# Level products two to five read 32 columns of R with a stride in place of all 64

## The chip, the cores and the metric

The kernel runs on one core of a Trainium2 chip. The metric is the device time of one execution in microseconds (us); lower is better. In what follows PE is TensorE, PEld its weight loads, DVE is VectorE, ACT is ScalarE, POOL is GpSimd and SP is SyncE, whose queue issues most DMAs.

## The reference

The kernel computes a linear attention with a decaying state and, on its output, a gated two-layer network. Batch is 4, heads 8, sequence 768, head dimension 48; the network has width 384 and 2048 hidden units. All is fp32.

```python
for t in range(S):
    cur = np.einsum('bhd,bhe->bhde', u[None] * kt, vt)
    y[:, :, t] = np.einsum('bhd,bhde->bhe', rt, state + cur)
    state = wt[:, :, :, None] * state + np.einsum('bhd,bhe->bhde', kt, vt)
# x: y as (3072 tokens, 384)
h = x @ w_in
sp = np.maximum(h, 0.0) + np.log1p(np.exp(-np.abs(h)))
out = (h * erf(sp)) @ w_out
```

So a query r of token t meets the key k of an earlier token s with all the decays w between them multiplied on.

## The kernel before

**Steps.** The work is cut into 12 steps: 6 chunks of 128 tokens times 2 pairs of batches. A step holds 16 heads (2 batches of 8). Two heads lie on each tile's partitions, the even head's 48 dimensions from partition 0 and the odd head's from partition 64, so that a tile has 8 such pairs (`n`) of 128 tokens. `in_t[:, 0]` is R (queries) and `in_t[:, 1]` is K (keys), both with tokens along the free dimension.

**Levels.** Inside a chunk each half of 64 tokens is treated by halving. At level l the tokens fall into blocks of 2^l; in each block the keys of the left half meet the queries of the right half. `scale` (L309, its instruction is at L332) multiplies the right halves of R and the left halves of K, in place, by the decays up to the middle of the block, so that at the next level the products carry the right decays. Per level, then:

- `level_products` (L536, matmuls at L544): for each of the 8 pairs, each half `s0` of the chunk and each of the two heads `e`, one matmul with 64 tokens of K as weights and tokens of R as the moving operand, into a PSUM tile `pp`. These are 32 matmuls, each of which the profile shows as two records with a weight load each. At levels 1 to 5 all 64 columns of K meet all 64 columns of R, at level 6 the left 32 of K meet the right 32 of R.
- `scale` for this level, on VectorE. It overwrites what the matmuls read, so it waits for them.
- `take_level` (L552): at levels 2 to 5 a masked copy on VectorE (L556) takes from `pp` the elements of this level into `own`, the 64 x 64 matrix of each head. It goes over the right halves of the columns only (`rights`, L52), 512 elements a partition, for `own`, for the mask and for `pp`. At level 6 ScalarE copies instead (L563). At level 1 the whole `pp` is multiplied by a mask (L896).

Steps 0 to 3 (`attend_first`, L739, and `attend`, L862) do levels 1 to 6; level 1 takes R and K with u multiplied in (`rk1`). Step 4 does levels 4 to 6, steps 5 to 11 (`attend_late`, L686) levels 5 and 6. There the low levels are done another way, by products on VectorE and POOL of rows of tokens (L467, L471) summed at L457, and `own` starts from these sums (L518).

Then `from_own` (L569, matmuls at L578) multiplies `own` by the values v, `through_state` (L592, L604) adds what comes from the state, and `state_part` (L643, L652) makes the new state. `spread_blocks` (L660, L665) is a small product of step 4 and later. `keep_busy` (L853, L857) issues matmuls of zeros in step 0.

**The network beside it.** The hidden layer (L1006) and the output layer (L1038 in the first steps, L1114 later) of earlier steps are cut into pieces, and pieces are put between the stages of the attention, in steps 1 to 4 by fixed tables (`STAGES`, `beside`, `in_order`), later by strings of tokens (`LATE`, `USUAL`). In steps 1 to 3 the weights are also brought into fp32, by ACT (L252, L254, L260), VectorE (L269, L274) and POOL (L282).

**Order.** All of this stands inside `tc.manual_schedule` for all five engines: each engine runs its instructions in the order in which the program names them, and waits only for what its operands need.

Of the kernel before, what the change touches and what calls it, by code (L numbers as in the profile page):

```python
# [20 lines left out]
HC = 64  # L21
# [22 lines left out]
MASKED = 5  # L44
# [7 lines left out]
def rights(ap, half):  # L52

    names = "abcdefg"[: len(ap.shape) - 1]
    spread = " ".join(names)
    return ap.rearrange(f"{spread} (n two h) -> {spread} n two h", two=2, h=half)[
        (slice(None),) * len(names) + (slice(None), 1)
    ]
# [3 lines left out]
def kernel(  # L62
# [237 lines left out]
    def rows(e, n=D):  # L300
        return slice(e * EP, e * EP + n)
# [234 lines left out]
    def level_products(pp, rk, level, ns=range(NJ * NP)):  # L536

        half = 1 << (level - 1)
        m = HC if level <= MASKED else half
        for n in ns:  # L540
            for s0 in range(0, C, HC):
                for e in range(NE):
                    t0 = s0 if level <= MASKED else s0 + half
                    nc.tensor.matmul(  # L544
                        pp[s0 : s0 + m, e, n, :m],
                        lhsT=rk[rows(e), 1, n, s0 : s0 + m],
                        rhs=rk[rows(e), 0, n, t0 : t0 + m],
                        start=True,
                        stop=True,
                    )  # L550

    def take_level(own, pp, level):  # L552
        half = 1 << (level - 1)
        got = pp[:].rearrange("p e n t -> p (e n) t")
        if level <= MASKED:
            nc.vector.copy_predicated(  # L556
                rights(own[:], half),
                rights(mask_sb[:, level - 1 : level, :].to_broadcast([P, NH, HC]), half),
                rights(got, half),
            )  # L560
        else:
            for s0 in range(0, C, HC):
                nc.scalar.copy(own[s0 : s0 + half, :, half:], got[s0 : s0 + half, :, :half])  # L563
# [122 lines left out]
    def attend_late(s, run):  # L686
# [4 lines left out]
        if before:  # L691
            from_own(before, ready[before][0], 1)
            fence()
        pp = products([P, NE, JP, HC], 0)
        level_products(pp, RK, LOG - 1)
        scale(s, LOG - 1)
        take_level(own, pp, LOG - 1)
        run("front", None)
        if before:
# [16 lines left out]

        pp = products([P, NE, JP, HC], 0)
        level_products(pp, RK, LOG)
        if s + 1 < n_steps:
            spread_blocks(s + 1, pp)  # L720
        take_level(own, pp, LOG)
        scale(s, LOG)
        run(1, following)
# [15 lines left out]
    def attend_first(xT):  # L739
# [11 lines left out]
        for half in halves:  # L751
            level_products(pp, made[:], 1, half)
            stay_warm(2)
# [17 lines left out]
        for level in range(2, LOG):  # L771
            pp = turns.pop("pp", None) or products([P, NE, JP, HC])
            level_products(pp, RK, level)
            scale(0, level)
            turns["pp"] = products([P, NE, JP, HC])
            keep_busy(turns["pp"])
            take_level(own, pp, level)
            if level in behind:
                wait_for(1 << level - 1)
                totals(*behind[level])  # L780
            if level == 2:
                stages["b"](0, 0)
                stages["b"](0, 1)
                stages["r"](0)
                for _ in prepare(1):
                    pass
                stages["l"](1, own[:, 0, 2:3])
                nc.sync.dma_start(out=vt[:], in_=v[0])
                nc.sync.dma_start(out=ws[1][:], in_=rkw[1][:, 2])
                load_w(2)  # L790
                load_v(1)
            elif level < LOG - 1:
                stages["h"](0)
# [455 lines left out]
    for kk in range(KT):  # L1249
        n = D // KT  # L1250
        to, of = (x.rearrange("p (e m) -> p e m", e=NE) for x in (apart[:, kk], ident[:]))
# [181 lines left out]
```

## Time and profile before

| | us |
|---|---|
| median of 3 runs (lowest, highest) | 592.12 (592.08, 592.5) |
| the profiled execution, its own time | 592.82 |
| its span, first to last instruction | 591.0 |
| TensorE busy | 581.3 |
| TensorE, level products (L544), records of 64 columns of K and of R from `in` | 29.0 |
| the same, level 6 | 9.1 |
| TensorE, hidden layer (L1006) | 256.9 |
| VectorE busy | 436.5 |
| VectorE, L332 with `tot_sb` | 82.0 |
| VectorE, L556, 25 copies, mean 0.813 | 20.3 |

The span is that of the profiled execution, in which times inside the trace are counted from the first instruction. A line of the groups names the line of the kernel, the engine, the operation, what is written and read, the shapes, the count, then busy time and mean duration (ns) and the idle time before it with what ended it. Matmul ends are modelled, and matmuls overlap, so the duration of one is not the time that it takes of the engine; starts are what to count with.

A matmul's shape in these groups is that of the weights with a star (48*64 is 48 rows and 64 columns) and that of the moving operand with an x (48x64 is 48 rows and 64 columns).

### The profile page before, as it was taken

What the parts mean: (1) busy time and instruction counts of PE and PEld (TensorE: products, weight loads), DVE (VectorE), ACT (ScalarE), POOL (GpSimd) and SP (SyncE); (2) the same over time, 40 slices, a digit from 0 to 9 for tenths busy, and PEclk for the clock granted to TensorE, in tenths of its full rate; (3) what the DMA queues carried; (4) which work ended last, traced back from release to release, by engine and by line L of the source; (5) the groups of instructions that cost most, each with busy time, mean ns of one, the idle gap of its engine ahead of it and who ended that gap; (6) DMA issues with size and microseconds to landing.
All of it is one profiled execution on the core that took longest, in us unless ns stands there. A gap on an engine that the chain in (4) does not pass through costs nothing.

```text
span 591.0 us, 16616 instructions
## 1 busy us (share of the span) xinstructions
PE 581.3 (98%) x7264; PEld 499.1 (84%) x7264; DVE 436.5 (74%) x518; ACT 361.3 (61%) x474; POOL 270.7 (46%) x305
## 2 busy tenths in 40 slices
PE   8899999999999999999999999999999999999997
PEld 6687887678668768998998998998898898898997
DVE  6686886899996899799799799799799525033140
ACT  3558877644544597766766766766766754746710
POOL 3466381702398479469369369369369000000000
PEclk9999999999999999999999999999999999999999
DMA  7786571440442514334334334333331300000000
GB/s 242 235 277 235 196 238 55 167 153 10 143 118 96 134 42 160 48 126 162 63 128 155 67 129 150 72 128 115 73 114 47 73 22 14 3 24 10 2 28 27
DMA packets 53937, 63.24 MB, mean 107 GB/s; under 512 B 35144, under 2 KB 40424, under 8 KB 52840
## 3 DMA queue, kind: packets, MB, share of 16 engines
q1 hardware_dynamic: 53480, 61.98, 33.3%
q8 instruction: 57, 0.93, 0.7%
q10 hardware_dynamic: 384, 0.20, 0.1%
q14 instruction: 16, 0.13, 0.1%
HBM read 52.39 MB, written 8.69 MB: 103 GB/s over the span
## 4 chain that ended last, share of the span: by engine, by line
PE 89%; ACT 4%; DVE 3%; issue 2%; DMA 1%; ACTq 0%; SPq 0%; DVEq 0%
PE m L1006 42%; PE m L1114 28%; PE pp L544 6%; PE m L1038 5%; PE y L578 2%; PE pp L652 2%; PE y L604 2%; DVE in L332 1%; ACT room L962 1%; PE pp L917 1%; ACT L966 1%; DMA u_sb<-in_u 1%; ACT L962 0%; DVE rk L467 0%; ACTq L638 0%
## 5 line engine op out<-in xcount | busy, mean ns | idle before, releaser
L1006 PE MATMUL m<-xT,w_in_sb 128*128 128x256 f32 x1152 | 256.9, 381 | 0.8 <-ACT o L1047 0.6
L1006 PEld LDWEIGHTS m<-xT,w_in_sb 128*128 128x128 f32 x1152 | 216.1, 190 | 31.7 <-ACT o L1047 1.0
L1015 ACT COPY h<-m 128x512 f32<-128x512 f32 x96 | 55.7, 580 | 83.7 <-PE m L1006 83.7
L332 DVE TENSOR_TENSOR in<-in,tot_sb 128x1024 f32<-128x1024 f32 (+1 forms) x59 | 82.0, 1390 | 17.0 <-PE pp L544 14.4
L467 POOL TENSOR_TENSOR rk<-words 128x528 f32<-128x528 f32 (+3 forms) x28 | 42.5, 1517 | 92.1 <-DVE sums L457 81.7
L471 POOL TENSOR_TENSOR words<-words,rest 128x528 f32<-128x528 f32 (+10 forms) x77 | 78.2, 1015 | 6.0
L1038 PE MATMUL m<-w_out_sb,h 128*128 128x384 f32 x192 | 64.3, 491 | 0.0
L1038 PEld LDWEIGHTS m<-w_out_sb,h 128*128 128x128 f32 x192 | 35.7, 190 | 23.6
L1114 PE MATMUL m<-mixed,h 128*128 128x192 f32 x288 | 51.1, 331 | 0.0
L1114 PE MATMUL m<-w_out_sb,h 128*128 128x192 f32 x288 | 50.3, 329 | 0.0
L962 ACT ACT_TABLE_LOAD x36 | 46.2, 1283 | 3.2 <-issue 2.5
L1114 PEld LDWEIGHTS m<-w_out_sb,h 128*128 128x128 f32 x288 | 46.9, 190 | 0.5
L1114 PEld LDWEIGHTS m<-mixed,h 128*128 128x128 f32 x288 | 46.6, 190 | 0.9
L966 ACT ACT_TABLE_LOAD x36 | 46.2, 1283 | 1.6 <-DVE room L1097 1.1
L1114 PE MATMUL m<-w_out_sb,room 128*128 128x192 f32 x256 | 44.2, 326 | 0.0
L544 PEld LDWEIGHTS pp<-in 48*64 48x64 f32 (+1 forms) x2368 | 33.6, 126 | 11.9 <-issue 6.5
L1114 PEld LDWEIGHTS m<-w_out_sb,room 128*128 128x128 f32 x256 | 42.0, 190 | 0.0
L971 DVE TENSOR_TENSOR h<-h,y 128x1024 f32<-128x1024 f32 x17 | 20.7, 1215 | 28.3 <-ACT y L966 28.2
L544 PE MATMUL pp<-in 48*64 48x64 f32 (+1 forms) x2368 | 38.0, 212 | 1.2 <-DVE in L332 1.0
L962 ACT ACTIVATE room<-h 128x1024 f32<-128x1024 f32 x36 | 38.1, 1057 | 0.4
L406 POOL TENSOR_TENSOR tot_sb<-tot_sb 128x256 f32<-128x256 f32 (+4 forms) x50 | 36.2, 723 | 3.8
L971 DVE TENSOR_TENSOR h<-h,pp 128x1024 f32<-128x1024 f32 x19 | 23.0, 1213 | 20.0 <-ACT pp L966 19.9
(141 smaller groups left out, 814.9 us busy)
## 6 DMA issues: line engine op xcount, KB each, us to landing
in<-in_rkw SPq DMA_DIRECT2D x8, 1024.0 KB, 5.4
words<-in_moe_w_in SPq DMA_DIRECT2D x16, 384.0 KB, 4.7
words<-in_moe_w_out SPq DMA_DIRECT2D x16, 384.0 KB, 4.3
words<-in_rk_rows SPq DMA_DIRECT2D x8, 768.0 KB, 6.4
w<-in_rkw SPq DMA_DIRECT2D x11, 512.0 KB, 5.7
v<-in_v SPq DMA_DIRECT2D x12, 384.0 KB, 5.9
out<-o SPq DMA_DIRECT2D x24, 192.0 KB, 3.3
in<-in_rkw SPq DMA_DIRECT2D x7, 512.0 KB, 5.3
```

Source lines behind the costliest of these rows:

```text
L332: nc.vector.tensor_mul(halves, halves, view(tots[level - 1], 0, [[1, n], [2, nb], [0, half]]))
L406: nc.gpsimd.tensor_mul(new, pair[:, :, 0], pair[:, :, 1])
L467: engine.tensor_mul(terms[n], r[:, :, n:], k[:, :, : near - n])
L471: engine.tensor_mul(k[:, :, :m], k[:, :, :m], w[:, :, n : n + m])
L544: nc.tensor.matmul(pp[s0 : s0 + m, e, n, :m], lhsT=rk[rows(e), 1, n, s0 : s0 + m], rhs=rk[rows(e), 0, n, t0 : t0 + m], start=True, stop=True,)
L962: nc.scalar.activation(sp_room, chunks[0], AF.Softplus)
L966: nc.scalar.activation(at, sp_room, AF.Erf)
L971: nc.vector.tensor_mul(h, h, at)
L1006: nc.tensor.matmul(ps[:, ff, :], lhsT=w_in_sb[:, g * FG + f + ff, kk * P : (kk + 1) * P], rhs=xT[:, kk, :], start=kk == 0, stop=kk == KT - 1,)
L1015: nc.scalar.copy(h[:, f : f + FT, :], ps[:])
L1038: nc.tensor.matmul(ps[j][:], lhsT=gs[g][:, f, j * C : (j + 1) * C], rhs=w_out_sb[:, g * FG + f, :], start=g + f == 0, stop=g == NG - 1 and ...
L1114: nc.tensor.matmul(to, lhsT=a[:, f], rhs=b[:, f], start=start and f == 0, stop=f == FG - 1, skip_group_check=True,)
```

## The change

The products of levels 2 to 5 take as moving operand the right halves of R's blocks alone: 32 of 64 columns, in runs of 2 tokens at level 2, 4 at level 3, 8 at level 4 and 16 at level 5, each run followed by a gap of the same length. The weights stay 64 columns of K. The 32 result columns are written side by side into the first half of each row of `pp`, and the masked copy reads them there; `own` and the mask are still addressed with the stride. Level 1 stays as it is. Level 6 goes through the same code and reads and writes what it did before. The number of instructions stays the same.

```diff
         for n in ns:
             for s0 in range(0, C, HC):
                 for e in range(NE):
-                    t0 = s0 if level <= MASKED else s0 + half
+                    right = rk[rows(e), 0, n, s0 : s0 + HC]
+                    to = pp[s0 : s0 + m, e, n, :]
+                    if level > 1:
+                        right = rights(right, half)
+                        to = to[:, : HC // 2].rearrange("p (b h) -> p b h", h=half)
                     nc.tensor.matmul(
-                        pp[s0 : s0 + m, e, n, :m],
-                        lhsT=rk[rows(e), 1, n, s0 : s0 + m],
-                        rhs=rk[rows(e), 0, n, t0 : t0 + m],
+                        to, lhsT=rk[rows(e), 1, n, s0 : s0 + m], rhs=right,
                         start=True,
                         stop=True,
                     )
...
             nc.vector.copy_predicated(
                 rights(own[:], half),
                 rights(mask_sb[:, level - 1 : level, :].to_broadcast([P, NH, HC]), half),
-                rights(got, half),
+                got[..., : HC // 2].rearrange("p n (b h) -> p n b h", h=half),
             )
```

## The prediction, made before the result

> **What bounds the kernel now.** I read the page first: who is busy, and what the chain that ended last is made of.
>
> ```profile
> PE 581.3 (98%) x7264; PEld 499.1 (84%) x7264; DVE 436.5 (74%) x518; ACT 361.3 (61%) x474; POOL 270.7 (46%) x305
> ...
> PE 89%; ACT 4%; DVE 3%; issue 2%; DMA 1%; ACTq 0%; SPq 0%; DVEq 0%
> PE m L1006 42%; PE m L1114 28%; PE pp L544 6%; PE m L1038 5%; PE y L578 2%; PE pp L652 2%; PE y L604 2%; DVE in L332 1%; ACT room L962 1%; PE pp L917 1%; ACT L966 1%; DMA u_sb<-in_u 1%; ACT L962 0%; DVE rk L467 0%; ACTq L638 0%
> ```
>
> TensorE is the bound: it is 89% of the chain, and the level products (L544) are 6% of it, some 35 us. So a level product that really becomes shorter makes the kernel shorter. The 7264 weight loads (PEld) stand beside 7264 matmuls: each matmul has a load of its own. The question is which of the two sets the pace in a level product. The groups of TensorE by shape (shape of the weights "rows*columns", shape of the moving operand, count, busy us, mean ns) show both kinds:
>
> ```profile
> L1006 PE MATMUL m<-xT,w_in_sb 128*128 128x256 f32 x1152 | 256.9, 381 | 0.8 <-ACT o L1047 0.6
> L1038 PE MATMUL m<-w_out_sb,h 128*128 128x384 f32 x192 | 64.3, 491 | 0.0
> L544 PE MATMUL pp<-in 48*64 48x64 f32 x1600 | 29.0, 220 | 1.0 <-DVE in L332 0.8 <-issue 0.2
> L652 PE MATMUL pp<-v,kT 64*48 64x48 f32 x704 | 12.3, 207 | 1.1 <-issue 0.9
> L665 PE MATMUL pp<-ident,over_blocks 48*64 48x48 f32 x28 | 2.2, 236 | 0.0
> ```
>
> ```profile
> L1006 PEld LDWEIGHTS m<-xT,w_in_sb 128*128 128x128 f32 x1152 | 216.1, 190 | 31.7 <-ACT o L1047 1.0 <-ACT y L254 0.5 <-DMA xT<-y 0.2
> L544 PEld LDWEIGHTS pp<-in 48*64 48x64 f32 x1600 | 25.8, 135 | 7.9 <-issue 3.9 <-DVE in L332 3.1 <-DVE own L556 0.5
> L652 PEld LDWEIGHTS pp<-v,kT 64*48 64x48 f32 x704 | 10.6, 121 | 4.5 <-issue 3.1 <-ACT y L1074 1.1 <-ACT m L252 0.3
> L544 PEld LDWEIGHTS pp<-in 48*32 48x32 f32 x768 | 7.7, 107 | 4.0 <-issue 2.6 <-DVE in L332 1.4
> ```
>
> A moving column costs (491 - 381) / 128 = 0.86 ns (384 against 256 columns). A column of weights costs (190 - 135) / 64 = 0.86 ns (128 against 64 columns); 121 and 107 for 48 and 32 lie on about the same line. So today a level matmul has a stream of 64 x 0.86 = 55 ns and a load of 64 x 0.86 = 55 ns, which run at the same time, the load for the next matmul under the stream of this one. The change halves the stream and leaves the load. The last matmul row is the witness that a load can be the longer one: L665 streams 48 columns against weights of 64, and a record of it is at least 218 ns by its line's view, where the median of L652, 48 columns against weights of 48, is 205: 13 ns more for 16 more columns of weights at the same stream, which is 16 x 0.86.
>
> The timeline of step 2 gives the length of whole products (start, us, then what), the first of 64 columns, the second (level 6, which takes 32 columns against weights of 32 already) of both halved:
>
> ```profile
> 70.49 1.16 PE L544 MATMUL pp<-in 48*64 48x64 f32 x64
> ...
> 71.58 0.70 PE L1006 MATMUL m<-xT,w_in_sb 128*128 128x256 f32 x2
> ```
>
> ```profile
> 82.12 0.76 PE L544 MATMUL pp<-in 48*32 48x32 f32 x64
> ...
> 82.81 0.48 PE L1006 MATMUL m<-xT,w_in_sb 128*128 128x256 f32 x1
> ```
>
> From start to the next piece: 1.09 us and 0.69 us. The 64 records go four at a time (two heads on different rows, two token halves on different columns), 16 turns. From the first start to the last it is 1.16 - 0.218 = 0.94 us, 59 ns a turn, which is one load or one stream with some 4 ns. The 0.40 us that level 6 is shorter belongs to load and stream together; it doesn't say what the stream alone would give.
>
> **What the Trainium skill says.** "TensorE: Matmul & The Clock Gate", section "LDWEIGHTS (loading the stationary operand)": the load's time goes by the columns of the weights, not by the rows. The trace agrees: 48 and 128 rows, and 107, 121, 135, 190 ns in the order of 32, 48, 64, 128 columns. The same page, "Step-by-step: what each phase is for": the load of the next weights is pulled ahead of the running matmul into a background buffer, matmuls stay in order. It speaks of one such buffer; the 59 ns turns fit with one load under one stream. "SBUF — State Buffer", section "Specifications (TRN2)": lines of 16 bytes, of which at least two accesses have to hit each for the full rate. Level 2 reads two fp32 of each four, just two hits; no row before shows a strided moving operand. The section "Who interferes with whom" of that page: GpSimd and a VectorE operation with two SBUF inputs exclude each other; the trace agrees, 2.53 us for L332 beside POOL's L282 where it takes 1.23 us alone.
>
> **The change, part by part.** Products of levels 2 to 5: four in each of steps 0 to 3, two in step 4, one in each of steps 5 to 11, 25 in all (1600 / 64). Levels 1 and 6 keep their shapes. No instruction, wait or DMA is added or moved.
>
> First, the halved stream. Each turn is the longer of load and stream: before max(55, 55), after max(55, 27.5). I take the turn as unchanged at 58 to 59 ns. What is left is the end: the last stream of a product has no load to wait for after it and ends 32 x 0.86 = 27 ns earlier, and with it the release of L332 and of the next piece of TensorE. Gross 25 x 0.027 = 0.68 us.
>
> What of it is on the path: a product counts if TensorE doesn't stand still later for something that was not waiting for that product. Step 0: TensorE sits idle 0.93 us ahead of L652 at 25.61, released by nothing that the profile shows; I count none of its four. Step 1: level 2 counts, levels 3 to 5 don't, because here VectorE and GpSimd set the pace:
>
> ```profile
> 42.34 0.69 DVE L556 COPY_PREDICATED own<-mask_sb,pp 128x512 f32<-128x512 int32 x1
> 42.93 2.53 DVE L332 TENSOR_TENSOR in<-in,tot_sb 128x1024 f32<-128x1024 f32 x1
> 45.39 0.94 DVE L269 TENSOR_SCALAR w_in_sb<-y 128x768 int32<-128x768 int32 x1
> ```
>
> ```profile
> 42.56 1.82 POOL L282 TENSOR_TENSOR w_in_sb<-w_in_sb,rest 128x768 int32<-128x768 int32 x1 [2.09 <-DVE w_in_sb L269]
> ```
>
> L269 releases L282 on POOL, L282 holds up L332 until 44.38, L332 ends 1.08 us later at 45.46, and the next product starts at 45.52. Step 2: level 2's gain is eaten by the wait of L1006 at 65.97 (0.46 us ahead of a load, put down to ACT L254), three count. Step 3: level 4's is eaten at 120.97, where TensorE waits 0.31 us for L332, behind a run of VectorE that begins at level 3's scaling; three count. Step 4: two. Step 5: none, TensorE waits 0.57 us at 224.31 for L1047, at the end of a run of ACT. Steps 6 to 11: one each, in stretches that are TensorE without a gap (44.53 of 44.53 us busy in the windows of whole steps). 15 x 0.027 = 0.41 us. Bounds: none, or all 25 (0.68).
>
> Second, the masked copy L556. Levels 3 to 5 take some 0.71 us for 512 elements a partition, level 2 takes 1.34 us (first one at 12.45). L332 at level 2 reads and writes SBUF in the same runs of two at 1.23 us for 1024 elements, so I lay the excess on the strided PSUM read, which the change makes contiguous. Bounds: nothing, or 1.34 - 0.71 = 0.63 us each for four copies; I take 0.63 off the copy, and 0 off the path. Its cover: in step 0 L332 at 13.88 starts 0.13 us after its own product's end (13.75), so it waits for TensorE, not for the copy; in step 1 it is held by L282 until 40.47; in steps 2 and 3 the TensorE pieces of 2.8 and 5.4 us lie over it. Without that cover it would be 4 x 0.63 = 2.5 us.
>
> Third, the moving operand read with a stride. Upper bound from the copy: runs of two cost it 1.34 / 0.71 = 1.9 times. 32 columns at 1.9 x 0.86 are 52 ns, still under the load. From below nothing. I take 0: what hides it is the load, and above 2.1 times (58 / 27.5) it would show.
>
> Sum: 0.41 us. The profiled execution is 592.82 us (span 591.0, 1.8 us around it); it would be 592.4. It lies 0.7 us above the median of the three runs, 592.12; from there 591.7.
>
> **The rivals.** A, the stream sets the pace after all (loads are pulled further ahead than one): a product falls to level 6's length, 0.40 us each. Steps 6 to 11 give 2.4, step 4 0.8, step 3 1.2, step 1 0.4. Step 2 gives some 0.2, since VectorE's four instructions per level (1.22 + 0.72 + 0.97 + 0.95 = 3.86 us) are as long as TensorE's 3.88. 5.0 us, 587.1. For it: level 6's row. Against it: L665, and that a load is seen per matmul. B, the copy of level 2 is on the path in steps 0 and 1: 2 x 0.63 + 0.41 = 1.7 us, 590.4. For it: the chain passes through L556 at 12.45; against it the 0.13 us above. C, slower: runs of two words slow the stream. It decides from 2.1 times; at 4 times a turn of level 2 is 110 + 5 ns in place of 58, 16 x 0.057 = 0.91 us a product, three in full (steps 0, 1, 3) and step 2's less the 0.25 us of slack there: 3.4 us, less 0.4: 595.1. For it: nothing before reads a strided stream; against it the two hits per line, and the 1.9 of the copy. That the edit does nothing measurable at all is the end of the likeliest case (592.1).
>
> **How the numbers follow.** Likeliest, the load bounds the turn: 0.82, 591.7 us, its own range 591.0 to 592.6 (all 25 on the path, or none, each with the 0.3 us or so by which runs differ, 592.08 to 592.5). A 0.09, B 0.04, C 0.05. The range takes in B: 590.4 to 592.6. A measurement here can tell 0.2%, 1.2 us, from no change. A and B are faster by more (0.13), C slower (0.05), the likeliest within (0.82).
>
> **What would show it.** L544's new group of 48*64 weights and 48x32 moving should show loads of 135 ns as before, and products of levels 2 to 5 some 1.06 us from start to the next piece in place of 1.09. Near 0.7, A is right; over 1.1, C. L556 at level 2 should be near 0.71 us; if it stays at 1.34, mask or output were its cause. The whole steps from 242.65 on should shrink by 0.03 us of 44.53. The forecast is wrong if TensorE's turn in these products isn't 58 to 59 ns.

## The result, and the profile after

| | before | changed |
|---|---|---|
| median (lowest to highest), 20 runs each | 592.2 us (591.53 to 596.48) | 591.87 us (590.6 to 598.44) |
| ratio, 95% interval | | 0.9998, 0.9976 to 1.002 |
| the profiled execution, its span | 592.82, 591.0 | 593.14, 591.4 |

No change that this measurement can tell, as forecast: 591.7 us, with 0.82 for "within 0.2%". Two later series of the same kernel gave 591.90 beside 592.12 and 591.65 beside 592.27, ratios 0.9994 (0.9979 to 1.0008) and 0.9994 (0.9981 to 1.0007).

In some executions of either kernel TensorE is granted half its clock for 3.4 us or more, in the profiled one of the changed kernel from 26.7 us on (the last section has the numbers), and this is one reason why runs spread over 5 us and more and why that execution is 1.3 us above its kernel's median. Its later stages, at full clock, can be compared with those of before.

These are the same views of the changed kernel, first the page's busy times and chain:

```profile
PE 582.7 (99%) x7264; PEld 500.7 (85%) x7264; DVE 434.8 (74%) x518; ACT 361.0 (61%) x474; POOL 271.8 (46%) x305
...
PE 90%; ACT 3%; DVE 3%; issue 2%; DMA 1%; ACTq 0%; SPq 0%; DVEq 0%
```

TensorE is still the bound. The groups by shape of the level products:

```profile
L548 PE MATMUL pp<-in 48*64 48x32 f32 x1600 | 28.0, 219 | 0.9 <-DVE in L332 0.6
L548 PEld LDWEIGHTS pp<-in 48*64 48x64 f32 x1600 | 25.7, 135 | 7.6 <-issue 4.0 <-DVE in L332 2.3 <-DVE own L558 0.5
L558 DVE COPY_PREDICATED own<-mask_sb,pp 128x512 f32<-128x512 int32 x25 | 20.4, 814 | 0.1
```

The moving operand is 48x32 now, half of 48x64. A record still takes 219 ns where it took 220, and the loads still take 135 ns each. The masked copy takes 814 ns in the mean, where it took 813. The timeline of step 2 (start, us, then what) has the length of a whole product:

```profile
71.03 1.14 PE L548 MATMUL pp<-in 48*64 48x32 f32 x64
72.09 0.70 PE L1008 MATMUL m<-xT,w_in_sb 128*128 128x256 f32 x2
```

1.06 us from its start to the next piece, in place of 1.09. And whole steps in the windows (from:to, length, then PE, PEld, DVE, ACT and POOL busy, granted clock, DMA share, GB/s), one of the kernel before and two of the changed one:

```profile
287.18:331.70 44.53, 44.53 (x533) 40.80 (x533) 40.28 (x50) 29.32 (x37) 27.87 (x33) 1.00 0.40 116
...
243.61:288.11 44.50, 44.50 (x547) 40.80 (x540) 40.30 (x50) 31.53 (x40) 28.58 (x34) 1.00 0.38 116
288.11:332.61 44.50, 44.50 (x547) 40.80 (x541) 40.15 (x50) 29.33 (x38) 27.87 (x33) 1.00 0.40 117
```

44.50 us, without a gap in TensorE, in place of 44.53: 27 ns for one product a step. One thing does not fit the forecast, the level 2 copy. The timeline of step 0 has it before, then in the changed kernel, there followed by the copy of level 3:

```profile
12.45 1.34 DVE L556 COPY_PREDICATED own<-mask_sb,pp 128x512 f32<-128x512 int32 x1
...
12.68 1.35 DVE L558 COPY_PREDICATED own<-mask_sb,pp 128x512 f32<-128x512 int32 x1
...
15.22 0.71 DVE L558 COPY_PREDICATED own<-mask_sb,pp 128x512 f32<-128x512 int32 x1
```

1.34 was to fall to 0.71 us with the contiguous read of PSUM, and it stayed.

### The profile page after: what moved, and what is told of

Same layout as the page of the kernel before. It is cut to its first block, busy times and chain, and to the rows that moved or that the text cites. A ratio compares the mean times of both kernels' runs of the same rounds, so it can differ in the third digit from the quotient of the medians.

```text
span 591.4 us, 16616 instructions
## 1 busy us (share of the span) xinstructions
PE 582.7 (99%) x7264; PEld 500.7 (85%) x7264; DVE 434.8 (74%) x518; ACT 361.0 (61%) x474; POOL 271.8 (46%) x305
## 4 chain that ended last, share of the span: by engine, by line
PE 90%; ACT 3%; DVE 3%; issue 2%; DMA 1%; ACTq 0%; SPq 0%; DVEq 0%
PE m L1008 43%; PE m L1116 28%; PE pp L548 6%; PE m L1040 5%; PE y L580 2%; PE y L606 2%; PE pp L654 2%; DMA in<-in_rkw 1%; ACT room L964 1%; PE pp L919 1%; ACT L968 1%; DVE in L332 1%; ACT L964 1%; DVE rk L467 0%; ACTq L640 0%
## 5 line engine op out<-in xcount | busy, mean ns | idle before, releaser
L332 DVE TENSOR_TENSOR in<-in,tot_sb 128x1024 f32<-128x1024 f32 (+1 forms) x59 | 80.5, 1364 | 16.5 <-PE pp L548 13.5
L548 PE MATMUL pp<-in 48*64 48x32 f32 (+1 forms) x2368 | 37.1, 212 | 1.1 <-DVE in L332 0.9
```

Source lines behind the costliest of these rows:

```text
L332: nc.vector.tensor_mul(halves, halves, view(tots[level - 1], 0, [[1, n], [2, nb], [0, half]]))
L548: nc.tensor.matmul(to, lhsT=rk[rows(e), 1, n, s0 : s0 + m], rhs=right, start=True, stop=True,)
```

## The experiments

My theory: a turn of four level matmuls is the longer of weight load and stream, the two are equal at 64 columns, so halving one of them alone does nothing. Rivals that also give an unchanged time: a stream of short strided runs costs twice as much per column and fills the time that its halving freed (then the weights don't matter), or a turn has a floor of 58 ns of another cause. All edits below are made to the changed kernel.

### Halving the weights as well: e1_w32_m32

```diff
+                    cut = HC // 2 if level > 1 else m
                     nc.tensor.matmul(
-                        to, lhsT=rk[rows(e), 1, n, s0 : s0 + m], rhs=right,
+                        to[:cut], lhsT=rk[rows(e), 1, n, s0 : s0 + cut], rhs=right,
...
+            few = slice(0, HC // 2)
             nc.vector.copy_predicated(
-                rights(own[:], half),
-                rights(mask_sb[:, level - 1 : level, :].to_broadcast([P, NH, HC]), half),
-                got[..., : HC // 2].rearrange("p n (b h) -> p n b h", h=half),
+                rights(own[few], half),
+                rights(mask_sb[few, level - 1 : level, :].to_broadcast([HC // 2, NH, HC]), half),
+                got[few, :, : HC // 2].rearrange("p n (b h) -> p n b h", h=half),
```

> Products of levels 2 to 5 with 32 columns of weights (the first 32 tokens of each half, so the products are of other keys, and the masked copy takes only partitions 0 to 31) and the strided 32 moving columns of the change. Theory (a turn of four records is the longer of weight load and moving stream; today the load of 64 columns): the turn falls from 58 ns to the 33 ns of level 6, a product from start to next piece from 1.06 to about 0.69 us, at all levels alike; the kernel gets 4 to 5 us faster, to about 587. Rival (the stride makes the stream slow, and the load hid it): level 2, with runs of two, shows a turn of 52 ns or more, levels 3 to 5 show 33. Rival (a turn has a floor of its own near 58 ns): nothing changes.

Measured: 589.69 us (7 runs) beside 592.85, ratio 0.9936 (0.9911 to 0.9961). The groups by shape of this kernel, level 6 included:

```profile
L549 PE MATMUL pp<-in 48*32 48x32 f32 x2368 | 28.2, 196 | 2.7 <-DVE in L332 2.6
L549 PEld LDWEIGHTS pp<-in 48*32 48x32 f32 x2368 | 24.0, 107 | 13.9 <-issue 6.1 <-DVE in L332 5.6 <-DVE own L560 0.7
```

Its timeline in step 2:

```profile
70.32 0.76 PE L549 MATMUL pp<-in 48*32 48x32 f32 x64
71.00 0.92 PE L1010 MATMUL m<-xT,w_in_sb 128*128 128x256 f32 x3
```

0.68 us for a level 3 product, as for level 6. Counted from start to start of every fourth record, the turn is 33 ns at levels 2, 3, 4 and 5 alike, that is for runs of 2, 4, 8 and 16 tokens, and at level 6, which has no stride. So the strided stream keeps up at half the turn that it has in the changed kernel, and the slow-stream rival falls: there is nothing that the stride costs. The gain, 3.2 us between the medians, is less than the 4 to 5 that the product lengths promised. The first row says where part of it went: TensorE now stands 2.6 us waiting for L332, in place of 0.9 in the changed kernel, level 6 included. The longest of these waits are 0.90 us in step 3 and 0.76 in step 4, where VectorE becomes the bound when TensorE's products shrink. In the late steps another part is lost: a step takes 44.28 us, 0.22 less than in the changed kernel, where the product alone became 0.33 shorter, because the level 5 product starts 0.11 us later behind L582's matmuls than before. No run tells why.

### Halving the weights alone: e2_w32_m64

```diff
-                    if level > 1:
+                    if level > MASKED:
                         right = rights(right, half)
...
+                    cut = HC // 2 if level > 1 else m
...
-                        to, lhsT=rk[rows(e), 1, n, s0 : s0 + m], rhs=right,
+                        to[:cut], lhsT=rk[rows(e), 1, n, s0 : s0 + cut], rhs=right,
...
```

> Products of levels 2 to 5 with 32 columns of weights (other keys, copy of partitions 0 to 31 alone, as in the run with 32 and 32) but the 64 moving columns of before. Theory: the stream of 64 columns sets the turn, 55 ns and 1 to 3 ns, so 56 to 58 ns as before the change, and a product takes 1.05 to 1.09 us; the kernel is within 0.2% of before. Rival (the load alone sets the turn, a stream costs nothing): 33 ns and 0.7 us.

Measured: 592.5 us in one run beside 592.85. The groups by shape (the loads with level 6), then the timeline of step 2:

```profile
L549 PE MATMUL pp<-in 48*32 48x64 f32 x1600 | 27.4, 218 | 1.1 <-DVE in L332 1.1
L549 PEld LDWEIGHTS pp<-in 48*32 48x32 f32 x2368 | 31.1, 107 | 12.4 <-issue 6.5 <-DVE in L332 4.4 <-DVE own L560 0.5
```

```profile
69.77 1.10 PE L549 MATMUL pp<-in 48*32 48x64 f32 x64
70.80 0.70 PE L1010 MATMUL m<-xT,w_in_sb 128*128 128x256 f32 x2
```

1.03 us a product and a turn of 56 ns, though each weight load is 107 ns in place of 135. This is the mirror of the change: half the load under a whole stream is worth as little as half the stream under a whole load. A late step even takes 44.62 us, 0.09 more than before, since here too the product starts 0.11 us later behind L582. The four cases together, with v1 below as a fifth:

| columns of weights, of moving operand | turn of four records, ns | first start to the next piece, us |
|---|---|---|
| 64, 64 (before) | 58 | 1.09 |
| 64, 32 (the change) | 58 | 1.06 |
| 32, 64 (e2) | 56 | 1.03 |
| 48, 32 (v1, v4) | 45 | 0.82 |
| 32, 32 (e1, level 6) | 33 | 0.68 |

Four of the lengths are from step 2; 48 by 32 is from the late steps, where the change's product takes 1.02 us. At 0.86 ns a column the longer of the two is 55, 55, 55, 41 and 28 ns; the turn is that and 1 to 5 ns. A fixed floor of 58 ns falls with the last two rows.

### Where the copy's excess lies: e5_psum_strided and e6_copy_operands

The first gives the result back its strided place in PSUM, so that the copy reads there with the stride as before, and keeps the 32 moving columns.

```diff
-                        to = to[:, : HC // 2].rearrange("p (b h) -> p b h", h=half)
+                        to = rights(to, half) if level <= MASKED else to[:, : HC // 2]
...
-                got[..., : HC // 2].rearrange("p n (b h) -> p n b h", h=half),
+                rights(got, half),
```

> The change with the 32 result columns written to PSUM where they stood before, with the stride, and read from there by the masked copy with the stride. Theory: the write is under the load too, turn 58 ns at all levels, copy of level 2 at 1.34 us as in both kernels, kernel as after the change (591 to 592). Rival (a strided PSUM write slows the matmul): level 2 shows turns well over 58 ns, and products over 1.1 us.

Measured: 595.11 us in one run, with TensorE at half clock for 6.83 us near 26 us, so its time says nothing; its rows do. Groups by shape, then the timeline of step 2:

```profile
L548 PE MATMUL pp<-in 48*64 48x32 f32 x1600 | 28.2, 219 | 1.0 <-DVE in L332 0.9
```

```profile
73.15 1.14 PE L548 MATMUL pp<-in 48*64 48x32 f32 x64
74.22 1.13 PE L1008 MATMUL m<-xT,w_in_sb 128*128 128x256 f32 x4
```

1.07 us, turns of 58 ns: under a turn that the load sets, writing PSUM in runs of two costs TensorE nothing. The level 2 copies take 1.33 to 1.37 us, as with the contiguous read. So the stride on PSUM's side adds nothing beside the strided `own`; a strided read of PSUM with `own` side by side wasn't tried.

The second keeps the changed products and varies the copy's own and mask operands, level 2 of step 0 as it is, of step 1 with the mask side by side, of step 2 with `own` side by side, of step 3 both.

```diff
+            side = lambda x: x[..., : HC // 2].rearrange("p n (b h) -> p n b h", h=half)
+            mask = mask_sb[:, level - 1 : level, :].to_broadcast([P, NH, HC])
+            kind = turns.setdefault("kind", -1) + (level == 2)
+            turns["kind"] = kind
...
-                rights(own[:], half),
-                rights(mask_sb[:, level - 1 : level, :].to_broadcast([P, NH, HC]), half),
-                got[..., : HC // 2].rearrange("p n (b h) -> p n b h", h=half),
+                side(own[:]) if kind in (2, 3) else rights(own[:], half),
+                side(mask) if kind in (1, 3) else rights(mask, half),
+                side(got),
```

> The changed kernel with the masked copies of levels 2 to 5 addressed differently by step, so that own takes elements at other places: step 0 as changed, step 1 with the mask read side by side, step 2 with own written side by side, step 3 with both. It asks what makes the copy of level 2 take 1.35 us in place of 0.71. If it is the read of the mask: 0.71 in steps 1 and 3. If it is the write of own: 0.71 in steps 2 and 3. If either alone is enough to slow it: 0.71 in step 3 only. The kernel's time stays within 0.2%, as the copy lies off the path.

Measured: 595.85 us in one run, again with 6.83 us of half clock. The level 2 copies of steps 1, 2 and 3 in its timeline (step 0's took 1.33):

```profile
41.42 1.33 DVE L562 COPY_PREDICATED own<-mask_sb,pp 128x512 f32<-128x512 int32 x1
...
71.93 0.74 DVE L562 COPY_PREDICATED own<-mask_sb,pp 128x512 f32<-128x512 int32 x1
...
109.85 0.73 DVE L562 COPY_PREDICATED own<-mask_sb,pp 128x512 f32<-128x512 int32 x1
```

The mask changes nothing, `own` side by side takes the whole excess away. It is the access to `own` in runs of two words; that it is the write alone isn't shown, as the copy might read `own` too. It isn't a property of all writes in such runs: L332 writes the same runs in SBUF, 1024 elements in 1.23 us.

The run also tells what a shorter copy is worth in steps 2 and 3, which ran at full clock: from the start of level 2's product to that of level 3 they take 6.87 and 6.42 us, in the changed kernel 6.88 and 6.42. There the copy is off the path.

### Where the small gain arises: e7_from_step1 and e8_step0_only

The change in steps 1 to 11 alone, and in step 0 alone.

```diff
-                    if level > 1:
+                    if level > MASKED or level > 1 and turns["cut"]:
...
-                got[..., : HC // 2].rearrange("p n (b h) -> p n b h", h=half),
+                got[..., : HC // 2].rearrange("p n (b h) -> p n b h", h=half)
+                if turns["cut"] else rights(got, half),
...
+            turns["cut"] = s > 0
```

(`not s` in the second.)

> The change in steps 1 to 11 only; step 0 as before. Theory: all of the counted gain lies here, 15 x 0.027 = 0.4 us; steps 6 to 11 take 44.50 us as in the changed kernel. If the lowered clock behind step 0 is made likelier by a faster step 0, it is rarer here than in the changed kernel, and the runs spread less upwards. Rival (the lowered clock has nothing to do with the change): the spread is as in both kernels.

> The change in step 0 only; steps 1 to 11 as before. Theory: step 0's products get 27 ns shorter each, but TensorE stands still near 25 us[...] and the gain is lost there: same time as before within 0.2%, steps 6 to 11 at 44.53 us. If a faster step 0 lengthens the standstill past some 1 us and so lowers the clock more often, the median lies up to 1 us above before.

Measured: 591.89 us (22 runs) and 592.42 us (14 runs) beside 592.12, ratios 0.9991 (0.9976 to 1.0007) and 0.9995 (0.9973 to 1.0016). The intervals hold both 0 and the expected tenths of a us; these times decide nothing. Nor do the runs without a lowered clock (a mean of 0.999 or more): the changed kernel has a median of 591.19 us there beside 591.71 in this series and 591.52 beside 592.15 in the other, about what was forecast, but e7, which has the change in all steps but the first, has 591.75. The traces decide for the late steps, which take 44.50 us in the first and 44.53 in the second. The clock isn't lowered more rarely in e7: it is in 4 of its 22 runs, in 3 of 14 of e8 and in 5 of 22 of the changed kernel in this series.

### Taking what the pair has: v1_w48_late, v3_w48_act, e9_w64_act, v4_w48_act_from6

A block's right queries meet only its left keys, so at level 5 the last 16 of 64 weight columns of each half are never needed. With 48 columns the load is 41 ns. The snag is that results then stand on partitions 0 to 47 and 64 to 111, so one masked copy becomes two.

v1 does this at level 5 in steps 4 to 11, with two masked copies:

```diff
+                    cut = m if level != MASKED or not turns.get("late") else HC - half
...
-                        to, lhsT=rk[rows(e), 1, n, s0 : s0 + m], rhs=right,
+                        to[:cut], lhsT=rk[rows(e), 1, n, s0 : s0 + cut], rhs=right,
...
+            parts = [slice(0, P)]
+            if level == MASKED and turns.get("late"):
+                parts = [slice(s0, s0 + HC - half) for s0 in range(0, C, HC)]
+            for of in parts:
...
+            turns["late"] = s >= DIRECT
```

> The changed kernel with the weights of level 5 cut to the first 48 columns of K in steps 4 to 11 (the last 16 tokens of each half are right halves of their block, and no element of level 5 has them as key); the masked copy of these levels goes over the 48 partitions of each half in two instructions. Theory: the turn follows the load, 48 x 0.86 and 4, so 45 ns in place of 58 with 32 moving columns; a late level 5 product gets 16 x 13 ns = 0.2 us shorter, a step of 44.50 becomes 44.29, and seven or eight steps give 1.4 to 1.7 us: about 590.3 where the changed kernel has 591.9. VectorE gets one copy of 0.7 us more per step, which its slack (40.1 of 44.5 us busy) covers. Rival: the second copy delays L332 and with it level 6, and gives the gain back: steps stay at 44.5 us.

Measured: slower, 595.52 us (22 runs) beside 592.12, ratio 1.0051 (1.0032 to 1.0069). Groups by shape, the timeline of one late step on VectorE, and of the same step on TensorE:

```profile
L549 PE MATMUL pp<-in 48*48 48x32 f32 x512 | 7.1, 205 | 0.0
L549 PEld LDWEIGHTS pp<-in 48*48 48x48 f32 x512 | 6.6, 122 | 0.5 <-issue 0.5
```

```profile
289.23 1.44 DVE L564 COPY_PREDICATED own<-mask_sb,pp 48x512 f32<-48x512 int32 x2
```

```profile
287.12 0.89 PE L549 MATMUL pp<-in 48*48 48x32 f32 x64
287.94 2.87 PE L1122 MATMUL m<-w_out_sb,h 128*128 128x192 f32 x16
...
310.02 13.44 PE L1014 MATMUL m<-xT,w_in_sb 128*128 128x256 f32 x60
323.66 8.04 PE L1014 MATMUL m<-xT,w_in_sb 128*128 128x256 f32 x36 [0.20 <-ACT h L1023]
```

The product did what was expected: loads of 122 ns, turns of 45 ns, 0.82 us from its start to the next piece. The whole step still takes 44.99 us in place of 44.50. The second copy is 0.72 us more on VectorE at 289.2. VectorE's later instructions of the network (L1099 to L1105) come 0.80 us later in the step by it, ACT's activations that read their result (the wait of ACT's L974 for `room`) with them, ACT's copy of the hidden layer L1023 behind those, and 36 us after the product TensorE waits for that copy, in front of 323.66. There the loads wait 1.0 us for L1023 in two waits, where the changed kernel has none. Its line in the waits of that step (engine, line waited for, sum, times, longest):

```profile
PEld m L1014 <- ACT h L1023: 1.0, 2, 0.6
```

From the start of L1014's 96 matmuls to the next piece it is 21.61 us, in the changed kernel 20.92. These 0.69 us less the product's 0.20 are the 0.49 by which the step is longer.

The rival of that expectation, a gain given back behind a busier VectorE, occurred, only by this route and not by L332.

v3 takes the copies to ScalarE instead: four copies of 16 partitions each after the first softplus, without a mask, in steps 5 to 11. e9 makes the same copies with all 64 weight columns. v4 is v3 from step 6 on.

```diff
+        if level == MASKED and turns.get("late"):
+            def take():
+                for s0 in range(0, C, HC):
+                    for i in range(2):
+                        of, at = s0 + 2 * half * i, half * (2 * i + 1)
+                        nc.scalar.copy(
+                            own[of : of + half, :, at : at + half],
+                            got[of : of + half, :, half * i : half * (i + 1)],
+                        )
+            turns["take"] = take
-        if level <= MASKED:
+        elif level <= MASKED:
...
+                turns.pop("take", lambda: None)()
...
+            turns["late"] = s > DIRECT
```

(The line of `cut` is v1's, `cut = m` in e9; `s > DIRECT + 1` in v4.)

> The weights of level 5 cut to 48 columns in steps 5 to 11, and the level's elements taken by four small ScalarE copies behind the first softplus of the step, in a stretch in which ScalarE waits 1.3 us for TensorE, with no masked copy on VectorE. Theory: the turn is 45 ns, a product 0.19 us shorter as in the run that did this with two masked copies, and VectorE, which lost that run its gain, is relieved of 0.7 us; a step of 44.50 us becomes about 44.31, six to seven of them 1.2 us, about 590.6 where the changed kernel has 591.9 (0.2% under it, 0.25% under before). Rival: ScalarE is as tight as VectorE was, and the four copies of about 0.4 us come back as waits of L1006 for its copy L1015; steps stay at 44.5 us or get longer.

> The same four ScalarE copies with the full 64 columns of weights. Theory: turn 58 ns as in the changed kernel, steps at 44.50 us, time as the changed kernel; so what the run with 48 columns gains over this one is the load's alone. Rival: moving the copy gains or loses by itself: steps differ from 44.50 us by more than 0.05.

Measured: v3 593.77 us (14 runs) beside 592.47, ratio 1.0008 (0.9991 to 1.0025); e9 593.81 (22 runs), ratio 1.002 (1.0009 to 1.0031). In v3 steps 6 to 10 take 44.30 us each, 0.20 less than in the changed kernel, as expected; in e9 44.50. But step 5 takes 47.37 us in v3 and 47.14 in e9, in place of 45.39 to 46.21 in the three profiles of the changed kernel. The timelines of TensorE in step 5, v3 first and then e9:

```profile
227.70 3.50 PE L1019 MATMUL m<-xT,w_in_sb 128*128 128x256 f32 x15 [2.05 <-ACT o L1060]
```

```profile
226.15 2.21 PE L1019 MATMUL m<-xT,w_in_sb 128*128 128x256 f32 x9 [1.62 <-ACT o L1060]
```

The wait that the prediction named in step 5 (0.57 us at 224.31, for ACT's copy of the output; in the changed kernel 0.45, 0.16 and none) grew to 2.05 and 1.62 us. Since e9 has it too, the four copies on ACT make it and not the 48 columns: in step 5 ACT is the bound, in steps 6 to 10 it isn't.

> As the run with 48 columns of weights and four ScalarE copies, but from step 6 on; step 5, where TensorE waited 2.1 us for ScalarE's L1047 copy behind the added ones, is as in the changed kernel. Theory: steps 6 to 10 at 44.30 us, step 5 back at about 46.2, and six products 0.19 us shorter give 1.1 to 1.2 us against the changed kernel: about 590.6 (590.0 where the clock stays at full speed). Rival: the wait of step 5 only moves to step 6, or the clock is lowered so often that the median doesn't show it.

Measured: 590.41 us (590.15 to 591.72, 8 runs) beside 592.27, ratio 0.997 (0.996 to 0.998): faster than before. Its windows of two late steps, then its copies in the timeline of one:

```profile
286.32:330.62 44.30, 44.30 (x546) 40.61 (x540) 39.73 (x49) 30.66 (x42) 27.83 (x33) 1.00 0.40 117
330.62:374.92 44.30, 44.30 (x546) 40.62 (x540) 39.69 (x49) 30.67 (x42) 27.82 (x33) 1.00 0.39 117
```

```profile
288.81 1.47 ACT L563 COPY own<-pp 16x256 f32<-16x256 f32 x4
```

TensorE is still busy 44.30 of 44.30 us: the 1.47 us of ACT hide completely here. Six steps of 0.20 are 1.2 us, which is what lies between this median and the changed kernel's 591.65 of the same series. Six of v4's 8 runs are below the lowest of the changed kernel's 13 (591.17), so the gain shows against both kernels, though v4 was run in one series alone.

## Why the prediction was right

**The turn (step one)** held to the nanosecond: 58 ns before and after, and e1, e2 and v1 show the rule behind it, the longer of load and stream. L665, the witness that a load can be the longer one, was the right row to lean on. What the prediction quoted of the Trainium skill, "TensorE: Matmul & The Clock Gate", section "Step-by-step: what each phase is for", the next weights loaded under the running matmul, fits with all five rows of the table. How far ahead they are loaded isn't shown by them: loads that need 55 ns a turn would pace a deeper buffer as well.

The time alone would not have carried this. The forecast range held anything from no product on the path to all 25, and the runs can't tell these apart; what confirms the mechanism is the turn, the length of the products, and e1, e2 and v1.

**The product's end** is 27 ns earlier as computed: 1.09 to 1.06 us, and 0.027 per late step.

**What of it reached the path** I took stage by stage from the first level product of one step to that of the next:

| step | before, us | changed, us | difference | predicted |
|---|---|---|---|---|
| 2 | 33.761 | 33.686 | -0.075 | -0.081 |
| 3 | 53.087 | 53.073 | -0.014 | -0.081 |
| 4 | 49.084 | 49.032 | -0.052 | -0.054 |
| 5 | 46.123 | 46.205 | +0.082 | 0 |
| 6 to 10 | 222.619 | 222.485 | -0.134 | -0.135 |

Step 3 failed in size: three products were to count, and two did. Those of levels 2 and 5 gave their 0.027 us each. Those of levels 3 and 4 lie in the stretch that a run of VectorE sets, from the start of level 3's product to that of level 5's, and this took 13.28 us before and 13.32 after: level 3's product released the run 0.03 us earlier, but the L332 that begins it took 1.31 us in place of 1.26. So TensorE waited longer in front of level 5, before and then after:

```profile
120.97 1.16 PE L544 MATMUL pp<-in 48*64 48x64 f32 x64 [0.31 <-DVE in L332]
...
121.44 1.14 PE L548 MATMUL pp<-in 48*64 48x32 f32 x64 [0.41 <-DVE in L332]
```

In step 5, bound by ACT, 0.08 us is nothing: three profiles of the changed kernel have 46.21, 45.39 and 45.68 us there. Steps 0 and 1 can't be compared in these two profiles, because of the half clock in one of them; in the two later ones of the changed kernel, at full clock, step 1 takes 33.69 and 33.70 us beside 33.67 before, so the one product counted there isn't seen. Without step 5 the rows sum to -0.28 us, and to -0.31 and -0.28 with the two later profiles, where -0.35 was forecast, all of it too small for the clocked times to tell.

**The copy (step two)** was wrong as to its cause and right as to its weight. "I lay the excess on the strided PSUM read" failed: in the change the read is contiguous and the copy takes as long as before, and e6 puts the whole 0.6 us on the access to `own`. It cost nothing, since the prediction had taken 0 for it on the path.

**The stride (step three)** was right at 0, and more safely than the bound said: the prediction needed the load to hide a cost up to 2.1 times, and e1 shows that with runs of two words there is no cost to hide, at a turn of 33 ns. The Trainium skill, "SBUF — State Buffer", section "Specifications (TRN2)", asks for two hits per line of 16 bytes, which level 2's runs just have; e1's trace agrees, with 33 ns at level 2 as at level 6, and a run of one word wasn't tried.

**The rivals.** A (the stream sets the pace) is refuted by the unchanged turn, C by e1. B (the copy on the path in steps 0 and 1) couldn't occur, since the copy did not shrink; e6 shows a shorter copy off the path in steps 2 and 3, but no run shows it in steps 0 and 1.

## What to carry to other kernels

In these products, small fp32 matmuls with new weights each time, load and stream overlap and the longer one is the turn. So in a kernel of this kind first compare the columns of weights with the columns of the moving operand: halving one of two equal sides bought only the end of the group, halving both took the turn from 58 to 33 ns. Before cutting a matmul's result to fewer partitions, price the extra copies on the engine that takes it over, and follow them through the later instructions of that engine: v1 lost more in a wait 36 us later than its product had won, and the same trim with the copies in ACT's idle time of steps 6 on won. To put an excess of an operation with three operands on one of them, vary one at a time; don't go by the one that looks unusual.

## What the runs showed of the hardware

**A standstill of TensorE of about 1 us can be followed by a window at half clock.** In step 0, within L652 (L654 after), TensorE stands for a time that no semaphore of the profile explains. In the timelines, before and then after:

```profile
25.61 0.61 PE L652 MATMUL pp<-v,kT 64*48 64x48 f32 x19 [0.93 <-issue]
...
27.41 0.68 PE L544 MATMUL pp<-rk 48*64 48x64 f32 x32
```

```profile
25.36 0.61 PE L654 MATMUL pp<-v,kT 64*48 64x48 f32 x19 [1.02 <-issue]
```

In the fourteen profiled executions, standstills there of up to 0.94 us were followed by the full clock, those of 1.02, 1.30 and 1.41 us (after, e9, e1) by 3.41 us at 0.5, those of 2.02 and 2.39 us (e6; e5 and v3) by 6.83 us at 0.5; one of 1.22 us (e8) kept the full clock, so the length alone doesn't decide. Later in the kernel standstills of 1.62 us (e9, step 5), 1.78 (e8, step 2) and 2.05 (v3, step 5) kept it too. At half clock the level 1 products turn in 107 ns instead of 58.

The Trainium skill, "TensorE: Matmul & The Clock Gate", section "What's actually happening", has a window of about 3.4 us and half clock behind an idle one, and calls the window free-running. The traces agree with the window: in all fourteen each change of the clock falls a whole number of 3.413 us after the start of the full clock, the half clock behind these standstills 20.48 us after it, which is six. They differ in that the window needn't be idle throughout. TensorE was busy 0.37 to 0.59 of the window with the standstill in the six executions that lost the full clock, and 0.62 or more of the windows there in the eight that kept it. Where the standstill falls in the window bears on this, as these lines show (third number from the end: the granted clock), the changed kernel's window and the next, then e8's:

```profile
23.30:26.71 3.41, 2.01 (x98) 1.65 (x88) 1.31 (x4) 1.42 (x4) 1.30 (x1) 1.00 0.94 334
26.71:30.13 3.42, 3.42 (x68) 3.03 (x69) 1.93 (x3) 1.12 (x2) 3.41 (x3) 0.50 0.19 72
...
21.67:25.08 3.41, 2.12 (x53) 1.73 (x53) 1.32 (x3) 1.75 (x4) 2.14 (x3) 1.00 0.95 338
25.08:28.49 3.41, 2.92 (x119) 2.60 (x119) 2.61 (x4) 1.78 (x3) 1.89 (x2) 1.00 0.46 165
```

The changed kernel's 1.02 us lie in one window; of e8's 1.22 us the last 0.16 lie in the next. The busy share isn't the whole rule either: in e8 the window from 66.04 us on was busy 0.53, and the full clock stayed. What else counts is open.

What makes TensorE stand there was not settled. The page lists a DMA queue of instructions (q8, 57 packets of 0.93 MB together before). In the thirteen executions with a standstill there (e7 has none), TensorE starts again 1.27 to 1.60 us after the end of a packet of 16384 bytes in this queue (24.29 and 25.61 us before, 23.95 and 25.36 in the changed kernel, 25.13 and 26.40 in e5). That it waits for instructions that come late is argued from this and not shown; no run changes when they come. Nor is it shown that the change makes the lower clock likelier or rarer: 15 of 55 runs of the changed kernel have it, and 27 of the 132 of before whose clock is listed.
